# Storing every other pair of output tiles through GpSimd's queue instead of all through SyncE's

## The chip, the cores and the metric

One core of one Trainium2 chip. The metric is the device time of the kernel in microseconds, as the median of several runs. Runs are compared with runs of the kernel before in the same rounds on the same chip. "Span" is the length of the one execution that the profiler recorded; it is some 1.8 us shorter than the time of that execution.

## The reference, cut to what matters

The kernel fuses linear attention over q, k, v of shape (8, 8, 576, 64) with a spectral mixer: Fourier transform along the sequence, 64 modes times complex 512 x 512 weights, inverse transform, then a residual with a channel product:

```python
Y[:, :n_modes] = Yr + 1j * Yi
y = np.fft.irfft(Y, n=S, axis=1)
u = x + y
return (u + np.maximum(u @ w_ch, 0.0)).astype(np.float32)
```

Only the last line matters here. Its output, 8 x 576 x 512 in float32, is 9.44 MB, and it has to be written to HBM at the very end, because the inverse transform needs the last mode's weights.

## The kernel before

Nearly all of the time goes into streaming the weights. When the last one has landed, the outputs are finished in one burst. There are 36 output tiles of 128 x 512, taken as 18 pairs. Pairs 0 to 3 are finished and stored tile by tile, pairs 4 to 17 pair by pair:

```python
    def store(t: int, n_t: int):
        if t < B * NJJ:
            b, jj = divmod(t, NJJ)
            r0 = b * S + BASE[b % 2]
            nc.sync.dma_start(
                out=out_rows[r0 : r0 + 512, :].rearrange("(r j) d -> r j d", j=NJJ)[:, jj : jj + n_t, :],
                in_=x_main[b][:, jj : jj + n_t, :],
            )
            return
        ...                                     # pairs 7 and 16: the same from x_tail
    def finish(n: int):
        acc = accs[n]
        t0 = pairs[n][0]
        add_inverse(n, 0)                                               # TensorE
        ...
        on_bank(n, {0, 1}, nc.vector.tensor_tensor(out=x, in0=acc, in1=x, op=ALU.add))   # VectorE
        ...
        store(t0, 2)                                                    # 512 KB
...
    for h, eng in enumerate((nc.sync, nc.gpsimd)):     # GpSimd's last work before the change
        eng.dma_start(out=YZ_all[64 * h : 64 * h + 64 : NF // NL]..., in_=last...)
...
    for n in range(5, len(pairs)):
        channels(n)
        rectified(n)                                                    # ScalarE: relu
        finish(n - 1)
    finish(len(pairs) - 1)
```

GpSimd's queue carries all weight loads. After the YZ_all half it has nothing more to do.

## Time and profile before

| | before |
|---|---|
| time, median of 5 | 421.46 us (421.16 to 421.89) |
| span of the profiled run | 419.57 us |
| first store issued | 391.67 us |
| VectorE's last addition ends | 414.18 us |
| last store lands | 418.41 us |
| end of span less end of VectorE | 5.39 us |
| GpSimd's closing drain | 390.54 to 399.04 us |

The kernel ends with a barrier (a point at which all engines wait for each other), the rows of line L1007: each engine's sequencer runs a DRAIN instruction and reports, SyncE after it has seen all transfers land. The one that reports last sets the end. Here that is SyncE, after the last store. "Landing" is the moment at which a transfer's semaphore is complete; "issue" is the record of the instruction that starts it.

### The profile page before, as it was taken

The page shows a single profiled execution, that of the slowest core. Times are in us where ns is not written, and L with a number is a line of the kernel's source. Part 1 is how long each engine was busy: PE and PEld are TensorE (multiplying, and loading weights), DVE is VectorE, ACT ScalarE, POOL GpSimd, SP SyncE. Part 2 cuts the span into 40 slices and gives each one's busy share as a digit, 9 for nine tenths or more (in the row PEclk, how much of TensorE's full clock was granted, in tenths as well). Part 3 has the DMA queues.
Part 4 walks back from the last instruction along what each step waited for, and adds up shares of the span by engine and source line. Part 5 has one row for each costly group of instructions (what it writes and reads, how often), then busy time and mean ns, then how long its engine had stood idle before and what let it go on. Part 6 is the DMA issues. An engine that isn't in the chain of part 4 may idle for free.

```text
span 419.6 us, 7400 instructions
## 1 busy us (share of the span) xinstructions
PE 288.7 (69%) x3115; PEld 155.9 (37%) x3115; DVE 228.6 (54%) x499; ACT 154.2 (37%) x253; POOL 58.1 (14%) x100
## 2 busy tenths in 40 slices
PE   0359799899517553444343685998798878899993
PEld 0247677787301221222121232433343324354421
DVE  4587979994404462464645353454455433512794
ACT  4677888954101011000000233344253422230782
POOL 4222224210001111111111111111111111130000
PEclk9999958989655555555555589799899989999997
DMA  8999999999999999999999999999999999998698
GB/s 219 211 212 216 210 221 206 229 206 222 222 217 212 213 223 211 216 222 209 220 220 205 225 220 205 225 215 209 224 217 208 225 216 209 223 205 162 230 395 328
DMA packets 17073, 93.17 MB, mean 222 GB/s; under 512 B 2112, under 2 KB 3024, under 8 KB 12880
## 3 DMA queue, kind: packets, MB, share of 16 engines
q0 software_dynamic: 12496, 81.48, 93.3%
q1 hardware_dynamic: 4544, 11.22, 7.2%
q8 instruction: 24, 0.39, 0.3%
q14 instruction: 9, 0.07, 0.0%
HBM read 163.93 MB, written 9.44 MB: 413 GB/s over the span
## 4 chain that ended last, share of the span: by engine, by line
DMA 65%; PE 19%; DVE 5%; issue 3%; ACT 3%; POOL 2%; DVEq 0%; ACTq 0%; POOLq 0%
DMA w<-in_moe_w_i_dram 52%; DMA pick_sb<-row_pick 8%; PE P L431 7%; DMA k<-in_k_dram 5%; PE acc L747 3%; PE acc L787 2%; PE kvp L256 2%; ACT ke L207 2%; POOL w L116 2%; PE eps L688 1%; DVE x L292 1%; DVE ke L220 1%; POOL w L128 1%; DVE k L214 1%; PE zl L418 0%
## 5 line engine op out<-in xcount | busy, mean ns | idle before, releaser
L431 PE MATMUL P<-w,xz 128*32 128x512 bf16 x496 | 48.3, 530 | 64.3 <-DMA w<-in_moe_w_i_dram 61.8
L448 ACT CAST ys<-P 128x512 f16<-128x512 f32 x15 | 8.8, 585 | 131.6 <-PE P L431 131.6
L116 POOL DMA_DIRECT2D w<-in_moe_w_r_dram x31 | 17.8, 575 | 244.2 <-PE P L431 240.7
L431 PEld LDWEIGHTS <-xz 128*32 128x32 bf16 x496 | 13.2, 115 | 85.5 <-DMA w<-in_moe_w_i_dram 56.9
L446 DVE CAST ys<-P 128x512 f16<-128x512 f32 x17 | 11.8, 691 | 53.5 <-PE P L431 53.5
L688 PE MATMUL eps<-wch,xTw 128*128 128x512 f16 x144 | 40.6, 409 | 0.0
L162 PEld LDWEIGHTS <-qT 64*128 64x128 f16 (+1 forms) x640 | 22.8, 124 | 31.7 <-issue 17.2
L671 ACT CAST x16w<-x_main 128x512 f16<-128x512 f32 x32 | 19.8, 618 | 37.7 <-DVE x_main L669 37.7
L669 DVE TENSOR_TENSOR x_main<-ya,x_main 128x512 f32<-128x512 f32 x32 | 22.0, 691 | 18.7 <-PE ya L665 18.5
L256 PE MATMUL kvp<-vpad,ke 32*128 32x130 f16 x576 | 23.3, 255 | 9.1 <-ACT qT L243 6.4
L441 DVE COPY xz<-xt_c 64x256 bf16<-64x256 bf16 x62 | 22.9, 370 | 12.1 <-PE P L431 11.3
L696 ACT CAST E<-eps 128x512 f16<-128x512 f32 (+1 forms) x40 | 21.2, 539 | 19.5 <-PE eps L688 19.5
L256 PEld LDWEIGHTS <-ke 32*128 32x128 f16 x576 | 21.4, 113 | 10.8 <-issue 8.9
L162 PE MATMUL nw<-kv,qT 64*128 64x65 f16 (+1 forms) x320 | 18.9, 240 | 9.5 <-DVE x_tail L632 4.5
L418 PE MATMUL zl<-wch,id 128*128 128x512 f16 x93 | 23.0, 380 | 0.0
L292 DVE TENSOR_TENSOR x<-num,rd 128x512 f16<-128x512 f32 x32 | 22.1, 692 | 1.1
L236 PE MATMUL qTp<-id,qe 128*128 128x128 f16 x144 | 14.3, 278 | 11.7 <-DVE qe L220 9.5
L632 DVE TENSOR_TENSOR x_main<-nw,rd 128x256 f32<-128x256 f32 x32 | 11.2, 417 | 17.3 <-PE nw L162 17.3
L207 ACT ACTIVATE qe<-q 128x1152 f16<-128x1152 f16 (+1 forms) x16 | 17.9, 1157 | 7.5 <-DMA q<-in_q_dram 7.4
L454 PE MATMUL yt<-pick_sb,ys 128*128 128x32 f16 (+1 forms) x128 | 8.8, 186 | 16.9 <-DMA pick_sb<-row_pick 10.7
L680 DVE COPY xTw<-xTp 128x512 f16<-128x512 f16 x36 | 15.0, 416 | 10.0 <-PE xTp L678 9.9
L243 ACT COPY qT<-qTp 128x1152 f16<-128x1152 f16 x16 | 19.6, 1291 | 0.5 <-PE qTp L236 0.2
(118 smaller groups left out, 494.6 us busy)
## 6 DMA issues: line engine op xcount, KB each, us to landing
w<-in_moe_w_r_dram POOLq DMA_DIRECT2D x31, 1024.0 KB, 12.5
w<-in_moe_w_i_dram POOLq DMA_DIRECT2D x31, 1024.0 KB, 16.7
out_dram<-x_main SPq DMA_DIRECT2D x12, 512.0 KB, 3.8
k<-in_k_dram POOLq DMA_DIRECT2D x8, 576.0 KB, 13.1
v<-in_v_dram POOLq DMA_DIRECT2D x8, 576.0 KB, 14.4
q<-in_q_dram POOLq DMA_DIRECT2D x7, 576.0 KB, 12.8
out_dram<-x_main SPq DMA_DIRECT2D x8, 256.0 KB, 3.8
q<-in_q_dram SPq DMA_DIRECT2D x2, 576.0 KB, 4.5
```

The lines of the kernel that those rows point to most:

```text
L116: nc.gpsimd.dma_start(out=w_in[p][half::2], in_=two.rearrange("g (r dc) e -> (g r) dc e", dc=NDW))
L162: mm = nc.tensor.matmul(num[hpo][orow, c0 : c0 + 65], qT[rows, hpp, h2, cols], kv_sb[rows, hpp, h2, :])
L207: pin(nc.scalar.activation(out=ev[:, c], in_=heads(nm, b, c), func=AF.Exp))
L256: nc.tensor.matmul(kv_ps[:, h2, 0:130], phi["k", b][r0 : r0 + 32, j // NJ, j % NJ].rearrange("p o d -> p (o d)"), vp[r0 : r0 + 32, :, j, 0 ...
L292: nc.vector.tensor_tensor(out=dst.rearrange("p (o c d) -> p o c d", o=2, c=4), in0=nv[:, :, :, 0:64], in1=rden.unsqueeze(3).broadcast_to([ ...
L418: pin(nc.tensor.matmul(last_ps[0], id16, wch16[:, 0, :]))
L431: nc.tensor.matmul(P[c : c + n, :], x, w[:, dc, :], start=(dc < NDC), stop=(dc >= n_dc - NDC), tile_position=(0, c), skip_group_check=True,)
L441: pin(nc.vector.tensor_copy(out=xz[p % 2][HALVES[h], :, h, :], in_=src))
L669: pin(nc.vector.tensor_tensor(out=x, in0=acc, in1=x, op=ALU.add))
L671: pin(nc.scalar.copy(out=x16w[t], in_=x))
L688: nc.tensor.matmul(e_ps, xT[:, c, :], wch16[:, c, :], start=(c == 0), stop=(c == NDC - 1))
L696: pin(nc.scalar.copy(out=dst, in_=e_ps[:, cols]))
```

## The change

The intent: with two queues, half of the stores need not pass through SyncE, so that issuing or landing overlaps better.

```diff
-    def store(t: int, n_t: int):
+    def store(t: int, n_t: int, eng=nc.sync):
...
-            nc.sync.dma_start(
+            eng.dma_start(
...
-        nc.sync.dma_start(
+        eng.dma_start(
...
-        store(t0, 2)
+        store(t0, 2, nc.gpsimd if n % 2 else nc.sync)
```

Seven stores of 512 KB move: pairs 5, 7, 9, 11, 13, 15 and 17. Pair 17 is the last store of the kernel.

## The prediction

> **What bounds the kernel now.** I read the page first: span 419.6 us, and the chain that ended last is 65% DMA, nearly all of it weight loads. The change does not touch those; it touches stores at the very end. So I went on with the chain in order of time, the busy time by window for the last 18 us, the list of SyncE's waits, the DMA issues, and at last the end-of-kernel line L1007, engine by engine.
>
> The last pieces of the chain of waits (start us, length us, what):
>
> ```profile
> 409.80 0.72 PE acc L747 x6
> ...
> 410.55 1.23 DVE x_main L821
> ...
> 411.82 1.23 DVE x_tail L821
> 413.05 1.13 DVEq L1007
> ```
>
> The last stretch is a run of VectorE additions of 1.23 us, the last of which ends at 414.2 (the last row is VectorE's sequencer draining behind it). What follows, 414.2 to 419.6, is the last store and the closing barrier. Busy time in that stretch (window; us; busy us of PE, PEld, DVE, ACT, POOL with counts; clock; DMA share; GB/s):
>
> ```profile
> 402.00:414.00 12.00, 10.45 (x57) 2.63 (x56) 11.92 (x11) 9.41 (x18) 0.00 (x0) 1.00 1.02 403
> 414.00:416.00 2.00, 0.00 (x0) 0.00 (x0) 0.18 (x1) 0.00 (x0) 0.00 (x0) 0.65 1.01 386
> 416.00:418.00 2.00, 0.00 (x0) 0.00 (x0) 0.00 (x0) 0.00 (x0) 0.00 (x0) 0.50 0.84 331
> ```
>
> From 402 to 414 two things are full at once: VectorE 11.92 of 12 us, and the 16 DMA engines at 1.02, with 403 GB/s, all on SyncE's queue. The DMA stays full until some 417 us. GpSimd does nothing. SyncE's waits there, and the issues with their landing times:
>
> ```profile
> SPq L803 <- DVE x_main L821: 9.1, 12, 0.9
> SPq L1007 <- DMA out_dram<-x_main: 2.3, 2, 1.2
> ...
> SPq L809 <- DVE x_tail L821: 1.7, 2, 0.9
> ```
>
> ```profile
> L803 SPq DMA_DIRECT2D out_dram<-x_main x8: 332/332/333, 403.4 to 411.8; - x8
> ...
> DMA to landing us min/median/max: 3.8/3.9/4.1
> ```
>
> SyncE needs 0.33 us for a store (least, median and most are in the row) and gets one only every 1.23 us; the rest of the time it waits for VectorE, up to 0.9 us per store. Its queue is about a quarter used. Nothing shows a store waiting behind another store's issue.
>
> The rows of the closing line L1007 up to 400 us and after 414.3 us (durations least/median/most in ns, then first and last start):
>
> ```profile
> L1007 POOLq DRAIN  x1: 8502/8502/8502, 390.5 to 390.5; - x1
> ```
>
> ```profile
> L1007 POOLq EVENT_SEMAPHORE  x4: 17/17/17, 418.8 to 419.5; - x4
> L1007 POOLq DRAIN  x2: 51/80/108, 419.0 to 419.3; - x2
> ```
>
> This is the row on which my prediction rests. GpSimd's last work now is one transfer of YZ_all at 390.57. Its sequencer goes straight on to the closing drain, starts it at 390.54, and the drain lasts 8.50 us, to 399.04. The same instruction with no fresh transfer before it takes 0.05 to 0.11 us. Today nobody notices: the barrier can't pass before SyncE has seen the last store land, at 418.4.
>
> **What the Trainium skill says.** "DMA: Bandwidth & Descriptors", section "Issuing engines are not separate DMA queues": transfers from every queue run on the same 16 engines and interleave, so a second queue saves only the sequencer's issue time. The trace agrees as far as it goes: one queue already has the engines at 1.02, and the issue time is 0.33 us out of 1.23.
>
> The same page, section "Latency and other measured facts": first byte some 600 ns on the hardware path (SyncE), some 1 us on the software path (GpSimd). The trace has one fair pair, the two halves of YZ_all, 256 KB each, issued at 390.30 and 390.57:
>
> ```profile
> YZ_all<-last SPq DMA_DIRECT2D x1, 256.0 KB, 3.2
> YZ_all<-last POOLq DMA_DIRECT2D x1, 256.0 KB, 3.9
> ```
>
> The packet records put the first packet 1.30 us after SyncE's issue and 1.97 us after GpSimd's; both ways the penalty is 0.7 us, more than the page's difference of 0.4.
>
> "SBUF — State Buffer", section "Who interferes with whom": a VectorE operation in a two-port mode can lock GpSimd out while it writes descriptors, one with at most one SBUF input outside such a mode does not. L821 reads PSUM and SBUF, so no lock is due. The YZ_all issue took 0.565 us with VectorE busy beside it, against 0.54 to 0.58 us for the last weight loads' issues: agrees.
>
> "Perfetto Trace Analysis", section "DMA Instruction — SWDGE (GPSIMD)": the record of such an instruction ends when the last descriptor is written, the cores finish their program later, unseen. The page gives no figure. Here the drain ended 7.9 us after the record (391.13) and 4.6 us after the landing (394.47). That the drain waits for this unseen part is my inference.
>
> **The change, part by part.** The helper gets a queue as argument. Eighteen pairs of tiles exist; the first four go through single-tile stores, which stay on SyncE. finish() runs for pairs 4 to 17; the odd ones, 5, 7, 9, 11, 13, 15, 17, move. That is seven stores of 512 KB, and the last store of the kernel, pair 17, is among them.
>
> Removed from SyncE: seven issues, 6 x 0.33 + 0.38 (pair 7 is an x_tail store) = 2.4 us. All lies in time in which SyncE waits for VectorE; worth 0 on the path.
>
> Added on GpSimd: seven issues of some 0.56 us, 4 us in all on an idle engine, worth 0. A GpSimd store comes every 2.46 us and needs four to five to land, so about two are in flight; weight loads back to back had seven, so no queue backs up.
>
> Moved transfers: the six before the last land some 0.9 us later (0.3 of later start, 0.7 of later first packet). No tile is used again, so nobody waits. The bytes and the 16 engines are the same.
>
> The last store: VectorE ends at 414.18. SyncE started 0.03 us later; GpSimd started the YZ_all half 0.30 us after its releaser (390.27 to 390.57), so 414.48. First packet 1.97 us later: 416.45. In the kernel before, the last store's packets began at about 416.4, because the engines were busy with the store before it. So most of the slower path is hidden behind that backlog, and the landing moves from 418.41 by 0.1 to 0.9, to about 418.8. With SyncE's end waits that alone would be +0.4 us.
>
> The drain: GpSimd's closing drain can't begin until this last transfer is issued, 414.45 with the same lead of 0.03. Add 8.50: 422.95. From 418.82, when GpSimd joined the barrier, to the span's end at 419.57 took 0.75 us: 423.70. Against 419.57 that is +4.1 us. If the drain counts from the landing instead, 418.8 + 4.57 + 0.75 = 424.1, +4.6. The landing's 0.4 us lies inside the drain and is not added. I take +4.1: 421.46 + 4.1 = 425.6 us.
>
> **The rivals.** First, a gain: two queues keep the engines fuller. For it: the share falls to 0.84 at 416 to 418, and early in the stretch it dips at 398 to 400. Against: 1.02 with one queue, VectorE at 11.92 of 12, and 0.33 us of issue. Even a store that landed at once could not end before VectorE's 414.2. The growth of landing time from 3.6 to 4.2 us over the stretch bounds the whole gain at 0.6 us: 420.9 us.
>
> Second, nothing but latency: the drain's 8.5 us belongs to that one transfer, or to housekeeping for the nine or so loads before it, and a later drain is short. For it: one drain is all that the trace has, and its end, 399.04, falls within 0.04 us of the landing of an unrelated store (399.01). Then only +0.1 to +0.9 remains: about 421.9 us. I give it one chance in six.
>
> Third, a longer drain: if each store leaves work behind and it adds up, seven stores could leave 10 to 20 us: 428 to 440 us. Against: issues 0.54 us apart show that a core is not held up for 8 us by each transfer, and a blocked load started 0.28 us after the landing it waited for. One chance in twelve.
>
> Fourth, the software queue's descriptor traffic slows the full engines. At 5% of the seven stores' 9 us that is 0.5 us, inside the drain. It does not show in the end.
>
> **Range and chances.** The middle is 425.6. The short-drain case sets the low end, 421.7; the high end, 428.0, leaves 2.4 us for a somewhat longer drain. Two per cent is 8.4 us: a gain of that size is impossible since only 5.4 us lie behind VectorE's end and 4.2 of them are the last transfer; a loss of that size needs a drain of 12.8 us or more. So 0.01 faster, 0.93 same, 0.06 slower.
>
> **What would show it.** Right: VectorE's last addition still ends near 414.2; the DMA share stays near 1.0; the last landing moves less than 1 us; L1007 has a GpSimd drain of about 8.5 us that starts near 414.5; SyncE and the others stand at the barrier until some 423. Wrong: a drain under 4 us there (the second rival), one well over 10 us (the third), VectorE ending later than 415 (the stores then reach back to compute, which I do not expect), or a landing after 420 (the queue itself is slow).

## The result and the profile after

The changed kernel took 426.44 us (426.10 to 428.15, five runs) against 421.46. The ratio is 1.013, with a 95% interval of 1.0109 to 1.0150: slower, by less than 2%. A ratio here compares the fast runs of both kernels in the same rounds, and it is not quite the ratio of the medians.

The closing line L1007 after 416.2 us, in the changed kernel (durations least/median/most in ns, then first and last start in us):

```profile
L1007 SPq EVENT_SEMAPHORE  x7: 28/28/5830, 415.5 to 421.7; - x7
L1007 SPq DRAIN  x2: 7/7/7, 421.8 to 421.8; - x2
L1007 POOLq DRAIN  x1: 9175/9175/9175, 416.4 to 416.4; - x1
```

The row to read against before's 8502 at 390.5 is the last. The drain now begins when the last store is issued, 416.40, lasts 9.18 us and ends at 425.58. SyncE is through with all its landings at 421.8 and then stands at the barrier. SyncE's waits show that, first in the kernel before, then in the changed one (us in total, times, longest us):

```profile
SPq L1007 <- PEq L1007: 0.7, 2, 0.5
```

```profile
SPq L1007 <- DMA out_dram<-x_main: 5.8, 1, 5.8
SPq L1007 <- PEq L1007: 4.5, 2, 4.0
```

The engine named, PE, had long been done; the wait of 4.0 us is the barrier's, and the drain is what was missing. The busy time by window, changed kernel (same columns as in the prediction):

```profile
416.00:418.00 2.00, 0.00 (x0) 0.00 (x0) 0.13 (x1) 0.00 (x0) 0.53 (x1) 0.83 1.00 389
418.00:420.00 2.00, 0.00 (x0) 0.00 (x0) 0.00 (x0) 0.00 (x0) 0.00 (x0) 0.50 1.03 391
420.00:422.00 2.00, 0.00 (x0) 0.00 (x0) 0.00 (x0) 0.00 (x0) 0.00 (x0) 0.50 0.32 125
422.00:424.00 2.00, 0.00 (x0) 0.00 (x0) 0.00 (x0) 0.00 (x0) 0.00 (x0) 0.50 0.00 0
424.00:426.40 2.40, 0.00 (x0) 0.00 (x0) 0.00 (x0) 0.00 (x0) 0.00 (x0) 0.50 0.00 0
```

From 422 on nothing moves and nothing computes, for over 4 us. The issues, with median time to landing, differ too; the kernel before had 3.8 us for the stores from x_main:

```profile
out_dram<-x_main SPq DMA_DIRECT2D x6, 512.0 KB, 4.6
out_dram<-x_main POOLq DMA_DIRECT2D x6, 512.0 KB, 5.5
```

Even the stores that stayed on SyncE land later.

**A trap in this pair of traces.** The spans differ by 6.8 us, not by 5. The profiled run of the changed kernel was its slowest, 428.15, and VectorE's last addition ended at 416.13 instead of 414.18. The shift of 1.95 us was there before the first store (391.67 against 393.61 us). Two windows ahead of the stores, before and then changed:

```profile
366.00:368.00 2.00, 2.00 (x14) 1.09 (x13) 0.86 (x3) 1.17 (x2) 0.00 (x0) 1.00 1.01 213
368.00:370.00 2.00, 1.91 (x28) 0.96 (x28) 0.00 (x0) 0.45 (x1) 0.24 (x1) 1.00 0.85 180
```

```profile
366.00:368.00 2.00, 2.00 (x6) 0.41 (x5) 1.18 (x2) 1.02 (x2) 0.00 (x0) 0.53 0.95 205
368.00:370.00 2.00, 2.00 (x9) 0.75 (x8) 0.86 (x3) 0.58 (x1) 0.00 (x0) 0.50 0.93 197
```

The third figure from the right is the granted TensorE clock: 1.00 there before, 0.50 to 0.53 in this run. TensorE does the same work in both kernels here, so I take this as chance and measure everything from VectorE's last addition. All thirteen traces bear that out: in five the granted clock of that first window was 0.50 to 0.53, and their first store came at 392.5 to 393.6 us; in the other eight it was 1.00, and the first store came at 391.6 to 391.8. One of the five, the last run below, has no store on GpSimd at all. From there to the end: 5.39 us before, 10.25 us after, so the change cost 4.86 us in the trace.

### The profile page after: what moved, and what is told of

It is laid out like the page before. It is cut to its first block, busy times and chain, and to the rows that moved or that the text cites. A ratio compares the mean times of both kernels' runs of the same rounds, so it can differ in the third digit from the quotient of the medians.

```text
span 426.4 us, 7400 instructions
## 1 busy us (share of the span) xinstructions
PE 290.4 (68%) x3115; PEld 155.8 (37%) x3115; DVE 228.7 (54%) x499; ACT 154.0 (36%) x253; POOL 61.9 (15%) x107
## 4 chain that ended last, share of the span: by engine, by line
DMA 59%; PE 19%; issue 8%; DVE 5%; POOL 3%; ACT 3%; POOLq 0%; ACTq 0%
DMA w<-in_moe_w_i_dram 48%; DMA pick_sb<-row_pick 8%; PE P L431 7%; DMA k<-in_k_dram 3%; PE kvp L256 2%; PE z L710 2%; DVE x L292 2%; ACT ke L207 2%; POOL w L116 1%; PE zl L418 1%; PE yp L723 1%; POOL out_dram L803 1%; PE yt L454 1%; ACT qT L243 1%; DVE rd L289 1%
## 5 line engine op out<-in xcount | busy, mean ns | idle before, releaser
L688 PE MATMUL eps<-wch,xTw 128*128 128x512 f16 x144 | 39.3, 399 | 0.0
L256 PE MATMUL kvp<-vpad,ke 32*128 32x130 f16 x576 | 22.5, 251 | 8.9 <-ACT qT L243 6.1
L418 PE MATMUL zl<-wch,id 128*128 128x512 f16 x93 | 24.0, 394 | 0.0
L162 PE MATMUL num<-kv,qT 64*128 64x65 f16 (+1 forms) x320 | 16.0, 214 | 5.8 <-DVE x L292 3.2
## 6 DMA issues: line engine op xcount, KB each, us to landing
v<-in_v_dram POOLq DMA_DIRECT2D x8, 576.0 KB, 14.4
```

Of the source, the lines that this page charges most:

```text
L162: mm = nc.tensor.matmul(num[hpo][orow, c0 : c0 + 65], qT[rows, hpp, h2, cols], kv_sb[rows, hpp, h2, :])
L256: nc.tensor.matmul(kv_ps[:, h2, 0:130], phi["k", b][r0 : r0 + 32, j // NJ, j % NJ].rearrange("p o d -> p (o d)"), vp[r0 : r0 + 32, :, j, 0 ...
L418: pin(nc.tensor.matmul(last_ps[0], id16, wch16[:, 0, :]))
L688: nc.tensor.matmul(e_ps, xT[:, c, :], wch16[:, c, :], start=(c == 0), stop=(c == NDC - 1))
```

## The experiments

Theory D: the loss is GpSimd's closing drain, which begins when its last transfer is issued. Rivals: the two queues slow each other's transfers (Q); the drain grows with the number of stores (N); the clock or something upstream (T). Eleven kernels ran. Each has a trace; small differences are read from it as two lengths, both from the end of VectorE's last addition: to the last landing, and to the end of the span. The stretch from the first store to that addition is 22.51 or 22.52 us in every trace except for the ScalarE one, so these lengths are steadier than the times: runs of the kernel before lie up to 2.3 us apart (421.16 to 423.41 us over all rounds). Its median was 421.46 us beside the first runs of the changed kernel and 421.61, 421.43 and 421.48 us in the three later sets.

| run | time, us | ratio to before (95%) | to last landing | to end |
|---|---|---|---|---|
| before | 421.46 | | 4.23 | 5.39 |
| changed, first trace | 426.44 | 1.0130 (1.0109 to 1.0150) | 5.20 | 10.25 |
| changed, again | 426.72 | 1.0109 (1.0093 to 1.0126) | 5.20 | 10.25 |
| only pair 17 | 425.62 | 1.0094 (1.0079 to 1.0110) | 4.32 | 9.63 |
| odd pairs to 15 | 424.23 | 1.0057 (1.0043 to 1.0071) | 5.18 | 8.21 |
| odd pairs to 9 | 422.49 | 1.0016 (1.0002 to 1.0030) | 4.91 | 6.26 |
| only pair 5 | 422.15 | 1.0018 (0.9996 to 1.0041) | 4.65 | 5.88 |
| only pair 11 | 421.84 | 1.0001 (0.9984 to 1.0018) | 4.26 | 5.49 |

**Again: the changed kernel once more.**

> The changed kernel once more, for the spread of its runs. Theory D (GpSimd's closing drain): 4.8 us over the kernel before, some 426.2 us, and the stretch from VectorE's last addition to the end 10.2 us as in the first trace, whatever the earlier part does. Rival T (the granted TensorE clock, or something upstream, costs the time): the stretch varies little but the difference to before varies by 2 us with the moment at which VectorE's last addition ends.

VectorE ended at 415.02 us this time, 1.1 us earlier than in the first trace, and everything behind it was the same to 0.01 us. T is out as the cause of the change's loss; the spread goes with the clock ahead of the stores.

**Only the last store on GpSimd.**

```diff
-        store(t0, 2, nc.gpsimd if n % 2 else nc.sync)
+        store(t0, 2, nc.gpsimd if n == 17 else nc.sync)
```

> Only the last of the fourteen pair stores (pair 17) goes through GpSimd. Theory D: nearly the whole loss is there, +4.1 to +4.8 us over before, with a drain of 8.5 to 9.2 us that starts at the last store's issue. Rival Q (the two queues slow each other's transfers): at most a seventh of it, under +1 us. Rival N (the drain grows with the number of stores on GpSimd): a drain clearly shorter than with seven stores, end at +1 to +3 us.

```profile
L1007 POOLq DRAIN  x3: 51/99/8570, 415.4 to 424.5; - x3
```

One store out of seven brings 4.24 of the 4.86 us, with a drain of 8.57 us. Its transfer lands almost as early as SyncE's did, 4.32 us after VectorE instead of 4.23. Q and N can't explain that.

**Odd pairs up to 15.**

```diff
+        store(t0, 2, nc.gpsimd if n % 2 and n <= 15 else nc.sync)
```

> Odd pairs up to 15 go through GpSimd, pair 17 back on SyncE: six stores moved, the last GpSimd issue some 2.4 us earlier than in the changed kernel. Theory D: the drain starts 2.4 us earlier and still ends after the last landing, so +2.1 to +2.6 us over before. Rival Q: six sevenths of the loss, +4 us. Rival that only the last store's landing matters: +0 to +0.3 us.

+2.8 us in the trace, +2.6 in the medians: somewhat above the top of what was expected. The last GpSimd issue is at 412.07, and the drain is 9.56 us long, longer than that of the changed kernel although fewer stores moved. So the drain is not a constant.

**Odd pairs up to 9.** As above with `n <= 9`.

> Only pairs 5, 7 and 9 go through GpSimd. Theory D: the last GpSimd issue is near 404.5 us, the drain ends near 413.5 us, before SyncE's last landing at 418.4, so it is hidden: 0 +/- 0.4 us against before. Rival Q: three sevenths of the loss, +2 us.

The drain ran from 404.96 to 414.20 and was hidden, as expected. Yet 0.87 us stayed, beyond the 0.4 that I had allowed: the last landing is 0.68 us late, the rest comes after it. Something in the transfers does cost. The busy time of three microseconds, counted so that the first store is at the same place, first before and then with pairs up to 9 on GpSimd:

```profile
399.67:400.67 1.00, 1.00 (x8) 0.24 (x7) 0.97 (x2) 0.86 (x3) 0.00 (x0) 1.00 1.01 399
400.67:401.67 1.00, 1.00 (x9) 0.26 (x6) 0.95 (x2) 0.95 (x2) 0.00 (x0) 1.00 1.01 406
401.67:402.67 1.00, 1.00 (x8) 0.26 (x6) 1.00 (x2) 0.90 (x2) 0.00 (x0) 1.00 1.03 414
```

```profile
399.83:400.83 1.00, 1.00 (x8) 0.24 (x7) 0.97 (x2) 0.85 (x3) 0.56 (x1) 1.00 0.86 348
400.83:401.83 1.00, 1.00 (x9) 0.26 (x6) 0.95 (x2) 0.95 (x2) 0.00 (x0) 1.00 0.64 258
401.83:402.83 1.00, 1.00 (x8) 0.26 (x6) 1.00 (x2) 0.90 (x2) 0.17 (x1) 1.00 1.00 397
```

The engines (second figure from the right) were dry for half a microsecond when the first GpSimd store was due. This made a theory E: at that moment there is no backlog, so the later start of GpSimd's transfer is idle time for the engines, and what they lose there they hardly make up, because VectorE feeds them at just their own rate.

**Only pair 5, and only pair 11.** Two runs with one moved store each, `n == 5` or `n == 11`, tell E from a cost per store.

> Only pair 5, the first of the moved stores, goes through GpSimd; the drain is over near 411 us and hidden. Theory E (the DMA engines have no backlog at that time, run dry for GpSimd's later start, and never make it up, because VectorE feeds them at just their own rate): one dip in the DMA share near the 9th us of the stores and most of the 0.7 us that three such stores cost, so the last landing +0.4 to +0.7 us after VectorE's last addition, 4.6 to 4.9. Rival (each store on the second queue costs its share, 0.1 to 0.23 us): 4.3 to 4.45 us.

> Only pair 11 goes through GpSimd, issued near 407 us instead of pair 5 near 400 us. By then the engines run behind VectorE by some 0.3 us (landing 3.84 us after issue in the kernel before, against 3.55 at the start of the pairs), so by theory E most of GpSimd's later start is covered: last landing 4.3 to 4.5 us after VectorE's last addition (before 4.23, with pair 5 moved 4.65), no dip below 0.9 in the DMA share. The drain ends near 416 and is hidden; end within 0.3 us of before. Rival (each store on the second queue costs the same wherever it stands): 4.6 us or more again.

Pair 5 alone: last landing 4.65 us after VectorE, +0.42, near the lower end of what E expects and outside of what a cost per store allows; so the first store carries most, not all, of the 0.68. Pair 11 alone: 4.26, +0.03, even less than I expected from E. In the microseconds after its issue the DMA share falls to 0.90 once and not below. The windows around the moved store, first with pair 5 moved (DMA share 0.84 and 0.66), then with pair 11:

```profile
399.60:400.60 1.00, 1.00 (x8) 0.23 (x6) 1.00 (x1) 0.85 (x3) 0.56 (x1) 1.00 0.84 340
400.60:401.60 1.00, 1.00 (x10) 0.26 (x6) 0.95 (x2) 0.91 (x2) 0.00 (x0) 1.00 0.66 266
```

```profile
408.47:409.47 1.00, 1.00 (x6) 0.11 (x2) 1.00 (x2) 0.88 (x3) 0.25 (x1) 1.00 0.90 352
```

The packet records of these two traces fit E. With pair 5 moved, SyncE's packets thinned out at 400.4 us and GpSimd's first began at 400.99, 0.6 us later. With pair 11 moved, SyncE's went on to some 409.3 and GpSimd's first began at 409.53. So the same operation in the same queue cost 0.4 us or nothing, and what differed was whether the engines had other work at that time. In the times the two runs can't be told apart (intervals of 0.9996 to 1.0041 and 0.9984 to 1.0018); this rests on one trace each.

**A second queue without GpSimd.** The odd pairs through ScalarE's queue:

```diff
+        store(t0, 2, nc.scalar if n % 2 else nc.sync)
```

> The odd pairs through ScalarE's queue, so two queues but no GpSimd. If the loss is GpSimd's drain and its slow start: none of either, so the last landing follows VectorE's last addition by 4.2 to 4.4 us as before, unless ScalarE, 3.5 of 4 us busy there, is held up by the stores that it has to wait for in order, in which case VectorE's last addition itself comes later: +0 to +2 us. If any second queue costs: the landing is late by 0.7 to 1 us with VectorE in time. If two queues gain: -0.3 us or better.

421.81 us against 421.43, ratio 1.0000 (0.9984 to 1.0016). There is no late drain and no gain either. ScalarE was held up by its stores (from 402 to 414 us TensorE waited 1.5 us for ScalarE's results, against 0.3 before), and VectorE's last addition came 24.54 us after the first store instead of 22.51. The last landing nevertheless came only 0.4 us later in the trace (418.82 against 418.41; 0.5 counted from the first store), because it followed VectorE by 2.71 us: the backlog was gone. The busy time of the stretch in that run:

```profile
402.00:414.00 12.00, 9.83 (x56) 2.96 (x55) 10.39 (x10) 9.36 (x18) 0.00 (x0) 1.00 0.97 384
```

VectorE is busy for 10.39 us here instead of 11.92, and the DMA share falls from 1.02 to 0.97. Two limits lie so close in this stretch that slack in one is taken up by the other. Since ScalarE was slowed, this run doesn't show what a second queue without any such side effect would give.

**Is it the drain by itself? A tiny transfer at the end.** In the kernel before, all stores on SyncE, one useless transfer of 8 KB is added:

```diff
     finish(len(pairs) - 1)
+    spare = wpool.tile([128, NDW, D], BF16, tag="w", bufs=W_KEEP, name="spare")
+    pin(nc.gpsimd.dma_start(out=spare[:, 0, 0:32], in_=x_main[B - 1][:, 2, 0:32]))
```

> The kernel before with all its stores on SyncE, and after the last addition one tiny GpSimd transfer (128 x 64 B into a dead tile), which moves no output. It lands some 2 us after its issue instead of 3.9 to 5.3. If the drain runs from the issue (record's end + 8 to 9 us), it lasts 8.5 to 9.2 us again and the kernel ends +4.2 us over before. If it runs from the landing (+4.1 to 4.6 us, as in six traces so far), it lasts 6.1 to 6.9 us and the end is at +1.8 to +2.4 us. If the bytes or the output stores mattered: 0.

425.46 us against 421.43, ratio 1.0086 (1.0066 to 1.0106). The closing line has the number L1009 here:

```profile
L1009 POOLq DRAIN  x3: 51/99/8558, 414.5 to 423.5; - x3
```

A transfer that moves no output costs 4 us. The other question stayed open: on engines full of stores it landed after 4.2 us, not after 2, so issue and landing were not told apart.

**The same with a large transfer behind it.**

```diff
+    pin(nc.gpsimd.dma_start(out=spare[:, 1:NDW, :], in_=w_in[LAST][:, 1:NDW, :]))
```

> As the run before, with a second GpSimd transfer of 1.97 MB between two dead tiles right behind the tiny one. It is issued 0.55 us later and lands some 5 us later than the tiny one, 7 to 8 us after its issue. If the drain runs from the issue: it ends 0.55 us later than in the run before, +4.8 us over before. If it runs from the last landing: drain of 11 to 13 us, end at +7.5 to +9 us.

431.31 us, ratio 1.0230 (1.0208 to 1.0253). The large transfer landed 9.55 us after its issue, later than I had estimated, and the drain lasted until after that. Its length and the end, 9.99 us later than before in the trace, lie above the ranges that I had given:

```profile
L1010 POOLq DRAIN  x3: 46/99/13623, 415.2 to 429.3; - x3
```

13.62 us, ending 4.05 us after the landing. A drain that runs from the issue alone is refuted.

**The same on idle engines.** Both halves of YZ_all on SyncE, and GpSimd's last transfer a tiny one near 389 us:

```diff
     last_pair()
+    probe = ystage.tile([128, 2 * B], F16, name="probe")
+    pin(nc.gpsimd.dma_start(out=probe, in_=Y8[:, 0, NL - 1, :]))
...
-    for h, eng in enumerate((nc.sync, nc.gpsimd)):
+    for h, eng in enumerate((nc.sync, nc.sync)):
```

> The kernel before with both halves of YZ_all on SyncE, and GpSimd's last transfer a tiny one near 388.6 us, when the DMA engines stand idle, so that it lands some 2 us after its issue. If the drain always ends 4.1 to 4.6 us after the landing: 6.1 to 6.7 us. If there is a floor of 7.9 to 8.0 us after the record's end, whatever the landing (as the five drains of 8.50 to 8.57 us suggest, whose transfers landed 3.4 to 4.2 us after issue): 8.5 us again, 6.5 us after the landing.

```profile
L907 POOL DMA_DIRECT2D probe<-Y x1: 558/558/558, 389.1 to 389.1; - x1
...
DMA to landing us min/median/max: 1.6/1.6/1.6
```

```profile
L1009 POOLq DRAIN  x3: 51/108/8493, 389.0 to 419.2; - x3
```

It landed after 1.6 us and the drain still took 8.49. A drain that runs from the landing alone is refuted too. All thirteen traces, sorted by the time to landing of GpSimd's last transfer:

| run | issue to landing | drain | drain's end after the record's end | after the landing |
|---|---|---|---|---|
| tiny on idle engines | 1.60 | 8.49 | 7.91 | 6.86 |
| only pair 5 | 3.45 | 8.57 | 7.99 | 5.10 |
| before, ScalarE's queue, wider stores | 3.90 | 8.50 to 8.51 | 7.91 | 4.57 to 4.58 |
| only pair 17 | 4.03 | 8.57 | 7.99 | 4.52 |
| only pair 11 | 4.20 | 8.57 | 7.99 | 4.35 |
| tiny at the end | 4.23 | 8.56 | 7.99 | 4.31 |
| changed, twice | 4.90, 4.91 | 9.18 | 8.62 | 4.25 |
| odd pairs to 9 | 5.13 | 9.25 | 8.66 | 4.09 |
| odd pairs to 15 | 5.33 | 9.56 | 9.01 | 4.21 |
| tiny and large | 9.55 | 13.62 | 13.07 | 4.05 |

Two regimes: up to a landing of 4.2 us the drain is 8.5 to 8.6 us, whatever the landing; from 4.9 us on it ends 4.05 to 4.25 us after the landing. No run lies between. All runs fit a drain that takes whichever is later. One rival is untested: every drain over 8.6 us came with several GpSimd transfers under way or a large one, so a late landing of one small transfer alone was not seen. What GpSimd does in that time no trace shows; that stays open.

**Wider early stores, an attempt at a better kernel.** In the kernel before, stores of pairs 1 to 3 merged from single tiles into pairs:

```diff
-        store(t, 1)
+        if n == 0:
+            store(t, 1)
+        elif i == 1:
+            store(pairs[n][0], 2)
```

> The kernel before, with six of its eight early single-tile stores (256 KB, packets of 2 KB) merged into three pair stores (512 KB, packets of 4 KB), all on SyncE. The ScalarE run suggested that the bytes and not VectorE set the end: VectorE's last addition was 2 us late there and the end only 0.4. If so, wider packets early save up to 0.5 us (345 to 395 GB/s in those 3 us against 405), end at -0.5 to 0 us. If VectorE's last addition sets the end, or the later start of three stores costs what the packets save: 0 to +0.3 us.

422.06 us against 421.48, ratio 1.0013 (0.9991 to 1.0036), no gain; in the trace the last landing is 4.18 us after VectorE's end instead of 4.23, but the end itself 5.52 instead of 5.39. No run beat the kernel before.

## Why the prediction was right, and where it was not

The time lay in the range, and the mechanism is the predicted one. Step by step:

- Nothing to gain at SyncE's issue or from a second queue: right. VectorE's 22.5 us stretch didn't change, and the ScalarE run, a second queue without GpSimd's cost, came out equal (though with ScalarE slowed, so it is weak evidence alone).
- The closing drain moves behind the last store and becomes the end: right. It was shown by one moved store (+4.24 us), by a tiny transfer that moves no output (+4.2 us in the trace), and by the dose: with the last GpSimd store at pair 15 and 17 the end comes 2.82 and 4.86 us later, and at pair 9 the drain is hidden.
- Its size, 8.50 us: too small, it was 9.18. The step that failed is the sentence that the landing's delay "lies inside the drain and is not added". That holds up to a landing of some 4.2 us after issue, and the store landed after 4.9. With only pair 17 moved (4.03 us, drain 8.57) the step is right.
- The last landing, "+0.1 to 0.9, to about 418.8", so +0.4 us: it was +0.97 in both traces. The step behind it was that of the six earlier stores "nobody waits". The engines do. I had looked at the backlog at the last store only, and at the first moved store there was none. With the six moved and pair 17 on SyncE, the landing was already 0.95 us late; pair 5 alone gave 0.42 us of it, and how the rest comes about no run shows. With only pair 17 moved the landing came +0.09 us later.
- The delay of those six, "some 0.9 us later (0.3 of later start, 0.7 of later first packet)", was taken from the two halves of YZ_all, which turned out to be no fair measure. In the trace with pair 5 moved, SyncE's store of pair 4 had its first packet 0.83 us after issue and GpSimd's store of pair 5 had it after 1.13: 0.3 us, not 0.7. From pair 9 to 15, the moved stores of the changed kernel still landed 5.3 to 5.7 us after their issue, where SyncE's had taken 3.8 to 4.0.
- The sum from VectorE's end to the end: 9.5 us was predicted (5.39 + 4.13), 10.25 was measured: 0.27 to the start of the drain, 9.18 drain, 0.80 barrier. Of the missing 0.7 us nearly all is the drain's.
- "VectorE ending later than 415" was to show the prediction wrong. It did end later, at 416.13 and 415.02, but this doesn't come from the moved stores: the run with wider early stores, all of them on SyncE, had 415.23. The sign was badly chosen, since that moment moves by up to 2 us with the granted clock ahead of the stores.
- Rivals: a gain, a drain that adds up over the stores, and a short drain did not come. A slower transfer (the fourth) did come, not inside the drain in the end. No run tests the cause given for it, descriptor traffic; 0.42 of the 0.97 us is traced to the later start at pair 5.

## What to carry to other kernels

Before moving a last transfer to another engine's queue, look at what that engine's closing drain costs after a transfer; the row is in the trace of a kernel whose drain is still hidden. Here GpSimd stores whose last issue was at 412.07 us (pair 15) or later set the end, and so did a transfer of 8 KB; the store at 408.16 us (pair 11) did not. From the drain of 8.57 us and the 0.79 us between its end and the kernel's, I estimate the limit at some 9.4 us before the end, and earlier for a transfer that lands late: the large one held the end until 14.4 us after its issue. The later start of the other queue cost nothing (0.03 us) where the transfer engines had a backlog and 0.42 us where they had none, so ask for the backlog at each moved transfer, not at the last one.

## What the Trainium skill lacked or had wrong

- "Perfetto Trace Analysis", section "DMA Instruction — SWDGE (GPSIMD)", says that the cores finish their program after the recorded end, but gives no time, and no page tells that the closing drain waits for it. Here: at least 7.9 to 8.0 us after the record's end, and 4.05 to 4.25 us after the landing where the transfer takes longer, in thirteen traces.
- "DMA: Bandwidth & Descriptors", section "Issuing engines are not separate DMA queues", names only what a second queue saves. Moving stores to GpSimd's queue cost 4.86 us here: 4.2 us for the last store alone, 0.4 us for one early store on engines without a backlog.
- The same page, section "Latency and other measured facts", has a first byte of some 0.6 us for the hardware path and 1 us for the software path, and doesn't say from which moment. Counted from the start of the issue's record, the first packets began after 1.30 and 1.97 us for the two halves of YZ_all, but after 0.83 us for SyncE's store of pair 4 and 1.13 us for GpSimd's store of pair 5: later than stated so counted, and a difference of 0.67 or 0.30 us where the page has 0.4.
